# Reordered small loads, value loads, weight halves and last two units, and six added products of ones, in a fused attention and two-MoE kernel

## The chip, the cores and the metric

The kernel runs on one core of one Trainium2 chip. The core has TensorE (PE, with its weight loads shown as a queue of their own, PEld), VectorE (DVE), ScalarE (ACT), GpSimd (POOL) and SyncE (SP), which issues nearly all of the plain DMA transfers here. The metric is device time in microseconds (us), the median over several executions.

## The reference

Three stages follow each other. All data is float32.

- Attention: q, k, v are [4 batches, 8 heads, 576 positions, 64]. Two attentions are added: one over positions averaged in groups of four (144 by 144, repeated to 576), and a local one in which a position sees those less than 4 away.
- First MoE (soft): with x = [2304, 512], `logits = x @ phi` (32 slots, 8 experts of 4 slots). A softmax over the 2304 rows mixes tokens into slots, each expert applies `relu(s @ w1[e]) @ w2[e]` (512 to 1024 to 512), and a softmax over slots mixes the results back.
- Second MoE (top 2 of 8): `x @ w_gate + log1p(exp(x @ w_noise)) * noise`, the best two experts of each token, a softmax over the two, and `out[token] += weight * (relu(x @ w1[e]) @ w2[e])`.

Each MoE has weights of 8 experts, two matrices of 2 MB per expert: 32 MB for each MoE.

## The kernel before, in words

**Attention by units.** A unit is one batch and two heads: 16 units, numbered 0 to 15. A software pipeline runs over p = -1 to 14. In step p the names of the list `SEQ` are called in order, each for the unit p minus its offset, so a unit's work is spread over several steps. What matters here: `ld` (line 187) loads k and q of unit p+2, four transfers of 144 KB; `A0`, `A1` (231) transpose k and q of unit p+1 on PE; `S` (284) makes the local scores of unit p, `SD` (298) the coarse ones; `M EL EX SU P0 P1` and `MD DX RD DM` are the two softmaxes; `VD` (267) averages the values of unit p-1; `CP`, `CD` transpose the probabilities; `DP` (408) and `DD` (420) multiply with the values; `XA`, `EP`, `LG`, `LA` add, transpose and make the router logits of unit p-2. `lV` (203) loads the values of unit p+1, mostly four transfers of 80 KB, into one of three buffers in turn. Every instruction order is written out by hand (`manual_schedule`): an engine runs its own instructions in the order in which the program calls them.

**The tail.** Units 13 to 15 are finished by the list `TSEQ`, with unit numbers written out (`DD:13`), which ends in the softmax over slots (`SE SK MT M4 SS ST MB QW QS UA DN UB SI`) and a few products of ones (`H2`, `H1`). `cp` (223) moves results from PSUM to SBUF, on DVE where the name is listed in `ON_V` (in the tail `ON_V_END`), else on ACT.

**Weights of the first MoE.** They are fetched during attention and after it. The 16 matrices go in the order `ORDW`. The first eight are loaded in steps 1 to 14: each matrix is four transfers of 512 KB, queued in a list, and at each name `W` (two per step) `NW[p]` of them are issued: 1 in steps 1 to 12, 2 in steps 13 and 14. The name `R2` in the tail (630) opens the second ring: three more matrices into space that the attention's own tiles leave, w8 and w10 (second matrices of an expert, in quarters: 8 transfers of 256 KB each) and w9 (a first matrix, 4 of 512 KB). A tile of the ring can be loaded when the attention tiles that lay there have been read for the last time. The last five matrices go into buffers of the first matrices once PE has used them (726 to 728). Then SP goes on to the second MoE's weights and to clearing the output (`clear`, 113).

SP issues all this from one queue, in program order. Ahead of the names of steps 13 and 14 stand four `small` loads each (596): the gate weights (`wgn`) and the noise (`nz`), in rows of 32 bytes.

**First MoE** (lines 794 to 857): `hidden`, `hidden_t`, `second` for eight experts on PE, accumulating in `yacc`.

**Second MoE.** After the router, DVE ranks the tokens and makes one-hot tiles `oh` (921). `dispatch` (934) multiplies them with the stacked token data `stk` into `xs0` and `xs1`. For expert 0 the first `NOH` = 10 dispatches run ahead of the expert's matmuls (1228), then `spin` (1089, products of ones that nothing reads), then `gathered` copies `xs0`, then first layer (1042) and `tile2` (1062), 24 matmuls of 512 columns for each 128 tokens. The weights of the second matrix are split in two parts, `whi` (ACT) and `wlo` (DVE), and so is the hidden layer, `hh` and `hl`.

Of the kernel before, what the change touches and what calls it, by code (L numbers as in the profile page):

```python
# [15 lines left out]

CAP = 640

SEQ = """ld DM S DD A0 M a00 a01 A1 W a110 XA a100 SD EL a101 ST a111 SK CP SS EX W VD EP01 MD V0 EP00 EP10 SU_ LG CD
EP11 EP V1 LA ED0 DX SU KD ED1 DP lV x1 x0 DQ1 X0 SE DQ0 RD P0 X1 P1""".split()  # L20
TSEQ = """S:15 DD:13 XA:13 DM:14 CP:14 W EP01:14 EP00:14 SD:15 M:15 EL:15 EP10:14 EX:15 EP11:14 CD:14 ED0:14 MD:15 SU:15 VD:14 DP:14 V0:14 V1:14 EP:13
ED1:14 P0:15 P1:15 DD:14 DX:15 LG:13 X0:13 RD:15 x0:14 DM:15 x1:14 CP:15 LA:13 EP00:15 X1:13 EP01:15 EP11:15
CD:15 EP10:15 XA:14 ED0:15 VD:15 DP:15 V0:15 V1:15 ED1:15 DD:15 EP:14 x0:15 x1:15 LG:14 X0:14 XA:15 LG:15 EP:15 X0:15 LA:14
LA:15 SE:3 X1:14 SK:2 H2 MT M4 X1:15 SS:3 H2 ST:3 MB R2 QW QS UA DN UB H1 SI H2 SK:3""".split()

ON_V = ['k1', 'd1', 'a101', 'a111', 'v0']
ON_V_END = ['P0', 'k1', 'v0', 'v1']

NW = [0] + [1] * 12 + [2] * 2

# [1 line left out]
NPRE = 8  # L32
NHOT = [4, 8]
N2 = 3
# [4 lines left out]
def attn_moe_moe_kernel(ctx: ExitStack, tc: tile.TileContext, q, k, v, moe_phi, moe_w1, moe_w2,  # L39
                        w_gate, w_noise, noise, w1, w2, out, dbg=None):  # L40
    nc = tc.nc
    B, H, S, D = q.shape
    NT = B * S
    DM = H * D
# [11 lines left out]
    NU = len(units)  # L56
# [13 lines left out]
    onesb = const.tile([128, 128], BF, name="onesb")  # L70
# [48 lines left out]
    with ExitStack() as tctx:  # L119
# [62 lines left out]
        def tp():  # L182
            return ps.tile([128, 512], F32, name="t", bufs=4)

        LD, KD, DQ, SD, SS, SB, PD, PL, XL, XT, XK = ({} for _ in range(11))
# [32 lines left out]
                    if j1 < 5:  # L218
                        nc.sync.dma_start(out=V[64:121, 4, h], in_=hv[h, S - 57:S])

        TAIL = []

        def cp(name, dst, src, alt=False):
            if name not in (ON_V_END if TAIL else ON_V) and not alt:
                nc.scalar.activation(dst, src, AF.Copy)  # L225
            else:
                nc.vector.tensor_copy(dst, src)
# [70 lines left out]
        def b_d(u):  # L298
            kd = KD.pop(u)
            sd = ps.tile([128, 512], F32, name="Sd")  # L300
            if u == 1:
                hot(NHOT[1], sd)
            for qb in range(3):
                nc.tensor.matmul(sd[0:96, qb * 144:qb * 144 + 144], Dq[:, qb].rearrange("p h i -> p (h i)"), kd,  # L304
                                 start=True, stop=True, skip_group_check=True)
            SD[u] = sd

        def soft_m(u):
            m = wka.tile([128, NG], F32, name="m")
# [128 lines left out]
        ET_ = {}  # L438
# [22 lines left out]

        def logit_pe(u):
            xT, kk = XT[u], u % 4
            L = SB[u + 2][:, 0:192] if not TAIL else ET_[u][1][:, 128:320] if u in ET_ else tp()[:, 0:192]
            for t in range(4):
                nc.tensor.matmul(L[32 * t:32 * t + 32, 0:128], phi[:, kk], xT[:, 128 * t:128 * t + 128],
                                 start=True, stop=True, skip_group_check=True)
            for t in range(4):
                nc.tensor.matmul(L[32 * t:32 * t + 32, 128:192], phi[:, kk], xT[:, 512:576], start=True, stop=True,
                                 skip_group_check=True)  # L470
            LL[u] = L

# [100 lines left out]
        MW, todo = {}, []  # L573

        def mload(i, pool, names=("wr", "wr")):
            MW[i], go = wload((moe_w1, moe_w2)[i % 2][i // 2], (4, 8)[i % 2], pool, names)
            if i == 2 * E - 1:
                go = [lambda f=f, c=c: f(ks=(c, c + 2)) for c in range(2) for f in go]
            todo.extend([lambda f=f, c=c: f(whole=c) for f in go for c in (1, 2)] if len(MW) <= NPRE else go)

        def flush(n=99):
            for _ in range(min(n, len(todo))):
# [2 lines left out]
        for i in range(NPRE):  # L585
            mload(ORDW[i], ringa if i < 3 else ringb)
        small = [(wgn[:, :, E * i:E * i + E], w.rearrange("(k p) e -> p k e", p=128))
                 for i, w in enumerate((w_gate, w_noise))]
# [4 lines left out]
        for p in range(-1, NU - 1):  # L593
            if p == 0:
                nc.sync.dma_start(out=phi, in_=moe_phi.rearrange("(k p) s -> p k s", p=128))
            for _ in range(4 if p >= NU - 3 else 0):
                o, i = small.pop(0)
                nc.sync.dma_start(out=o, in_=i)
            if p == 1:
                nc.gpsimd.memset(zero, 0.0)  # L600
            b4, r4 = divmod(p - 5, 4)
            for nm in SEQ:
                f, off, a = BL.get(nm, (None, 99, ()))
                if off is None:
                    if 0 <= b4 < B and r4 == a:
                        f(b4)
                elif ok(p - off):
                    f(p - off, *a)
                if nm == "W" and p >= 0:
                    flush(NW[p])  # L610
                if p == -1 and nm == "lV":
                    nc.gpsimd.memset(PT, 0.0)
                    nc.gpsimd.memset(Vd[:, 1], 0.0)
                    nc.gpsimd.memset(PdT[:, 1], 0.0)
                if p == -1 and nm == "DQ1":
                    nc.vector.memset(P, 0.0)
            if p == 0:
                hot(NHOT[0])
                nc.vector.tensor_scalar(trib, jp, 0.0, None, op0=ALU.is_gt)
                consts()  # L620
# [58 lines left out]
        for nm in TSEQ:  # L679
            if nm in TB:  # L680
                TB[nm]()
            elif nm[0] == "H":
                hot(int(nm[1:]))
            else:
                n, u = nm.split(":")
                f, off, a = BL[n]
                f(int(u), *(a if off is not None else ()))


# [244 lines left out]
    def dispatch(e, n):  # L934
        i = ORD[n]
        lo, hi = WIN[i]
        if n == 0:
            XP[e] = [ps.tile([128, n], F32, name=f"xs{c}", bufs=1) for c, (_, n) in enumerate(CH)]
        oh = OH.pop((e, n))
        c1 = CH[1][0]  # L940
        if lo < c1:
            nc.tensor.matmul(XP[e][0][:, lo:min(hi, c1)], stk[:, i], oh[:, 0:min(hi, c1) - lo], start=(n == 0),  # L942
                             stop=True, skip_group_check=True)
        if hi > c1:
            nc.tensor.matmul(XP[e][1][:, max(lo, c1) - c1:hi - c1], stk[:, i], oh[:, max(lo, c1) - lo:hi - lo],  # L945
                             start=(i == FIRST1), stop=True, skip_group_check=True)
# [139 lines left out]
        if (e, ti) in DRAINS:  # L1086
            nc.gpsimd.drain()  # L1087

    def spin(n):

        t = ps.tile([128, DM], F32, name="y") if n else None
        for _ in range(n):
            nc.tensor.matmul(t, onesb, onesb[:, None].to_broadcast([128, 4, 128]), start=True, stop=True)


    ELSE = {}
# [12 lines left out]
    with ExitStack() as gctx:  # L1109
# [13 lines left out]
        t = ps.tile([128, 2 * E], F32, name="h")  # L1123
# [9 lines left out]
        for q_ in range(5):  # L1133
            n = min(4, NTILE - 4 * q_)
# [69 lines left out]
        for i in range(NTILE - 1):  # L1204
            n = NTILE - 1 - i
# [21 lines left out]
            wsplit(0, kk, "v", (1,))  # L1227
        for n in range(NOH):
            dispatch(0, n)
        spin(SPIN[5])  # L1230
        gathered(0, (0,))
        if PLP is None:
# [178 lines left out]
```

## Time and profile before

| | us |
|---|---|
| three runs, median (lowest to highest) | 491.67 (491.55 to 493.74) |
| the profiled execution | 490.25 |
| span of its trace | 488.5 |
| PE busy, share of the span | 462.5, 95% |
| DVE, ACT, POOL busy | 275.3, 270.5, 220.1 |

Attention runs to about 158 us, the first MoE to about 193, the router to 204, and the rest is the second MoE. In tables by stage, the columns are the stretch, its length, busy us and instruction counts of PE, PEld, DVE, ACT and POOL, then the granted TensorE clock as a share of 2.4 GHz, the mean busy share of the 16 DMA engines (it can pass 1.00), and GB/s. In a timeline a row is the start, us, engine, line, operation, destination and source, the count, and in brackets the idle time before it with what ended it. SPq is SP's queue; its rows show when a transfer is issued, not when it lands.

### The profile page before, as it was taken

The numbers are of one execution on the slowest core, as the hardware profiler recorded it, in microseconds if no ns is written. First come the engines' busy times: TensorE is split into PE (matmuls) and PEld (weight loads), VectorE is DVE, ScalarE is ACT, GpSimd is POOL, SyncE is SP. The second block draws the span as 40 slices with busy tenths as digits, with TensorE's granted clock in tenths as the row PEclk, the third lists the DMA queues.
The fourth block names the chain that finished last, engine by engine and source line by source line (L and its number), as shares of the span: only waits on it lengthen the run. The fifth ranks groups of instructions, "written<-read, shape, count | busy, mean of one in ns | idle before, by whom it ended". The sixth has DMA issues, their size and how long they took to land.

```text
span 488.5 us, 12466 instructions
## 1 busy us (share of the span) xinstructions
PE 462.5 (95%) x4765; PEld 358.7 (73%) x4765; DVE 275.3 (56%) x703; ACT 270.5 (55%) x699; POOL 220.1 (45%) x321
## 2 busy tenths in 40 slices
PE   6999999899789999999999999999999999999992
PEld 5798788788575443577777887887887877878882
DVE  6888878878575321876578464383552634615300
ACT  2688877778483112665384464682755646727410
POOL 7898777678331001084556577322222222212232
PEclk9999999999799999979999999999999999999998
DMA  8999999999989999999977843799867855333333
GB/s 163 213 208 257 213 245 216 205 264 186 251 250 333 397 389 395 375 345 335 377 186 203 230 68 67 190 363 280 273 88 214 214 127 144 45 43 45 44 44 46
DMA packets 108233, 104.19 MB, mean 213 GB/s; under 512 B 67978, under 2 KB 77898, under 8 KB 108170
## 3 DMA queue, kind: packets, MB, share of 16 engines
q1 hardware_dynamic: 101258, 90.50, 62.5%
q0 software_dynamic: 6912, 12.85, 17.5%
q8 instruction: 40, 0.66, 0.6%
q14 instruction: 23, 0.19, 0.1%
HBM read 83.60 MB, written 19.73 MB: 212 GB/s over the span
## 4 chain that ended last, share of the span: by engine, by line
PE 58%; DMA 16%; issue 12%; SPq 3%; DVE 3%; ACT 3%; POOL 2%; POOLq 2%; ACTq 0%; DVEq 0%
PE y L1062 35%; DMA wr<-in_moe_w_dram 7%; DMA ld<-in_q_dram 5%; SPq L192 3%; PE t L237 3%; PE gx L879 2%; PE S L293 2%; PE h L1042 2%; PE Sd L304 2%; POOL out_dram L1081 2%; DMA V<-in_v_dram 2%; DMA w10b<-in_moe_w_dram 1%; POOLq L1087 1%; PE gx L1042 1%; PE xs L942 1%
## 5 line engine op out<-in xcount | busy, mean ns | idle before, releaser
L1062 PE MATMUL y<-whi,hh 128*128 128x512 f32 x320 | 127.6, 399 | 0.3 <-ACT hh L1043 0.3
L1062 PE MATMUL y<-whi,hl 128*128 128x512 f32 x320 | 127.7, 399 | 0.0
L1062 PE MATMUL y<-wlo,hh 128*128 128x512 f32 x320 | 127.3, 398 | 0.0
L1081 POOL DMA_INDIRECT out_dram<-ys,idx x40 | 63.9, 1597 | 110.3 <-ACT ys L1073 61.2
L1073 ACT ACTIVATE ys<-y,gt 128x512 f32<-128x512 f32 x40 | 27.4, 685 | 82.4 <-issue 47.1
L1062 PEld LDWEIGHTS y<-wlo,hh 128*128 128x128 f32 x320 | 60.5, 189 | 13.0 <-issue 0.8
L1034 DVE TENSOR_TENSOR wlo<-wr,whi 128x512 fp32r<-128x512 f32 x64 | 42.0, 692 | 49.5 <-ACT whi L1031 38.0
L1062 PEld LDWEIGHTS y<-whi,hh 128*128 128x128 f32 x320 | 60.7, 190 | 12.0 <-ACT hh L1043 0.6
L1062 PEld LDWEIGHTS y<-whi,hl 128*128 128x128 f32 x320 | 60.6, 189 | 11.5 <-issue 2.1
L1008 POOL DMA_INDIRECT tab<-stk,pos x36 | 35.8, 994 | 11.5 <-issue 10.4
L1044 DVE SCALAR_TENSOR_TENSOR hl<-h,hh 128x256 fp32r<-128x256 f32 (+1 forms) x64 | 31.3, 490 | 16.5 <-ACT hh L1043 14.3
L1044 DVE SCALAR_TENSOR_TENSOR hl<-gx,hh 128x256 fp32r<-128x256 f32 (+1 forms) x64 | 31.3, 488 | 11.1 <-ACT hh L1043 8.5
L1031 ACT ACTIVATE whi<-wr 128x512 fp32r<-128x512 f32 x64 | 36.9, 625 | 0.2
L1043 ACT ACTIVATE hh<-gx 128x256 fp32r<-128x256 f32 (+1 forms) x64 | 28.1, 439 | 16.0 <-PE gx L1042 13.2
L1043 ACT ACTIVATE hh<-h 128x256 fp32r<-128x256 f32 (+1 forms) x64 | 27.9, 436 | 13.5 <-PE h L1042 10.7
L237 PE MATMUL t<-idf,ld 96*128 96x96 f32 x192 | 23.5, 271 | 10.8 <-DMA ld<-in_k_dram 7.3
L1080 POOL MEMSET spacer<- 1x1 f32 x40 | 13.6, 339 | 42.4 <-issue 42.4
L255 POOL TENSOR_TENSOR s<-Q 64x288 f32<-64x288 f32 x31 | 29.3, 944 | 2.4
L237 PEld LDWEIGHTS t<-idf,ld 96*128 96x128 f32 x192 | 18.8, 154 | 15.0 <-issue 6.2
L337 POOL TENSOR_TENSOR P<-El,su 64x350 f32<-64x350 f32 x31 | 24.4, 786 | 11.3 <-DVE su L330 5.4
L225 ACT ACTIVATE PT<-t 64x384 f32<-64x384 f32 (+1 forms) x64 | 25.9, 428 | 3.1 <-PE t L379 1.9
L927 DVE TENSOR_TENSOR oh<-iot,R 128x256 fp32r<-128x256 f32 (+2 forms) x50 | 20.7, 447 | 11.5 <-PE xs L945 7.8
(312 smaller groups left out, 882.3 us busy)
## 6 DMA issues: line engine op xcount, KB each, us to landing
wr<-in_moe_w_dram SPq DMA_DIRECT2D x72, 512.0 KB
wr<-in_moe_w_dram SPq DMA_DIRECT2D x88, 256.0 KB
out_dram<-zero SPq DMA_DIRECT2D x20, 256.0 KB
V<-in_v_dram SPq DMA_DIRECT2D x62, 80.0 KB
ld<-in_k_dram SPq DMA_DIRECT2D x32, 144.0 KB
ld<-in_q_dram SPq DMA_DIRECT2D x32, 144.0 KB
XT<-tab SPq DMA_DIRECT2D x5, 320.0 KB
tab<-zero SPq DMA_DIRECT2D x6, 256.0 KB
```

Source lines behind the costliest of these rows:

```text
L225: nc.scalar.activation(dst, src, AF.Copy)
L237: nc.tensor.transpose(t[:, 96 * c:96 * c + 96], ld[:, i, 3 * j + c].rearrange("p h d -> p (h d)"), idf[0:96, 0:96])
L255: nc.gpsimd.tensor_tensor(q2, q4[:, :, 0:2], q4[:, :, 2:4], op=ALU.add)
L337: eng.tensor_tensor(P[as_, :, HQ * a:HQ * a + KW], El[as_], su[as_, :, None].to_broadcast([64, NG, KW]), op=ALU.mult)
L1008: st = nc.gpsimd.indirect_dma_start(out=tab, out_offset=bass.IndirectOffsetOnAxis(ap=pos[:, c, i:i + 1], axis=0), in_=stk[:, i].bitcast(F3 ...
L1031: nc.scalar.activation(whi[:, kk], wb(kk), AF.Copy)
L1034: eng.tensor_tensor(wlo[:, kk], wb(kk), whi[:, kk].bitcast(F32), op=ALU.subtract)
L1043: nc.scalar.activation(hh[:, f], h, AF.Relu)
L1044: nc.vector.scalar_tensor_tensor(hl[:, f], h, 0.0, hh[:, f].bitcast(F32), op0=ALU.max, op1=ALU.subtract)
L1062: nc.tensor.matmul(y, l[:, kk, ts_], r_[:, kk], start=(m == 0), stop=(m == 23))
L1073: nc.scalar.activation(ys, YS.pop((e, ti)), AF.Copy, scale=gt[:, ti:ti + 1])
L1081: st = nc.gpsimd.indirect_dma_start(out=out, out_offset=bass.IndirectOffsetOnAxis(ap=idx[:, ti:ti + 1], axis=0), in_=ys, in_offset=None, c ...
```

## The change

- In each step `lV` moves from behind `DP` to behind `A1`; the first `W` moves from behind `A1` to behind `CD`. SP's order in a step was k and q, weights, weights, values; it becomes k and q, values, weights, weights.
- The `small` loads of steps 13 and 14 move from ahead of the step's names to behind them.
- w8 and w10 are loaded in halves of a tile (512 KB) where they were loaded in quarters (256 KB): 12 transfers for the second ring where there were 20.
- `TSEQ` has another order. The logits of units 13 to 15 are put into the score banks `S` and `Sd` instead of the `t` buffers. The evacuations on DVE in the tail are listed by name and unit: `v1` (units 14, 15) goes to ACT; `p10`, `d1` and `x0` of unit 15 go to DVE.
- `spin` takes a width; behind each of the dispatches 4 to 9 of expert 0 stands one product of ones of 128 columns.

```diff
-SEQ = """ld DM S DD A0 M a00 a01 A1 W a110 XA a100 SD EL a101 ST a111 SK CP SS EX W VD EP01 MD V0 EP00 EP10 SU_ LG CD
-EP11 EP V1 LA ED0 DX SU KD ED1 DP lV x1 x0 DQ1 X0 SE DQ0 RD P0 X1 P1""".split()
-TSEQ = """S:15 DD:13 XA:13 DM:14 CP:14 W EP01:14 EP00:14 SD:15 M:15 EL:15 EP10:14 EX:15 EP11:14 CD:14 ED0:14 MD:15 SU:15 VD:14 DP:14 V0:14 V1:14 EP:13
-ED1:14 P0:15 P1:15 DD:14 DX:15 LG:13 X0:13 RD:15 x0:14 DM:15 x1:14 CP:15 LA:13 EP00:15 X1:13 EP01:15 EP11:15
-CD:15 EP10:15 XA:14 ED0:15 VD:15 DP:15 V0:15 V1:15 ED1:15 DD:15 EP:14 x0:15 x1:15 LG:14 X0:14 XA:15 LG:15 EP:15 X0:15 LA:14
-LA:15 SE:3 X1:14 SK:2 H2 MT M4 X1:15 SS:3 H2 ST:3 MB R2 QW QS UA DN UB H1 SI H2 SK:3""".split()
+SEQ = """ld DM S DD A0 M a00 a01 A1 lV a110 XA a100 SD EL a101 ST a111 SK CP SS EX W VD EP01 MD V0 EP00 EP10 SU_ LG CD W
+EP11 EP V1 LA ED0 DX SU KD ED1 DP x1 x0 DQ1 X0 SE DQ0 RD P0 X1 P1""".split()
+TSEQ = """DD:13 W S:15 CP:14 SD:15 EP01:14 XA:13 EP11:14 VD:14 M:15 EP00:14 EL:15 EX:15 EP10:14 MD:15 V0:14 V1:14 DM:14 CD:14
+SU:15 EP:13 DP:14 P0:15 ED0:14 ED1:14 X1:13 DX:15 P1:15 RD:15 DD:14 x0:14 CP:15 x1:14 LG:13 DM:15 X0:13 XA:14 EP11:15
+EP01:15 EP10:15 EP00:15 VD:15 CD:15 V0:15 V1:15 DP:15 ED1:15 ED0:15 LA:13 DD:15 x1:15 LG:14 EP:14 x0:15 XA:15 LG:15
+LA:14 X0:14 LA:15 SE:3 EP:15 X1:14 X1:15 X0:15 SK:2 H2 MT M4 SS:3 H2 ST:3 MB R2 QW QS UA DN UB H1 SI H2 SK:3""".split()
...
-ON_V_END = ['P0', 'k1', 'v0', 'v1']
+ON_V_END = ['P0', 'k1:13', 'v0:14', 'p10:15', 'd1:15', 'v0:15', 'x0:15', 'k1:14', 'k1:15']
...
-            SD[u] = sd
+            SD[u] = SB["d"] = sd
...
-            L = SB[u + 2][:, 0:192] if not TAIL else ET_[u][1][:, 128:320] if u in ET_ else tp()[:, 0:192]
+            L = (SB[min(u + 2, NU - 1)] if u < NU - 1 else SB["d"])[:, 0:192]
...
-            todo.extend([lambda f=f, c=c: f(whole=c) for f in go for c in (1, 2)] if len(MW) <= NPRE else go)
+            todo.extend([lambda f=f, c=c: f(whole=c) for f in go for c in (1, 2)] if len(MW) <= NPRE + N2 else go)
...
-            for _ in range(4 if p >= NU - 3 else 0):
-                o, i = small.pop(0)
-                nc.sync.dma_start(out=o, in_=i)
...
+            for _ in range(4 if p >= NU - 3 else 0):
+                o, i = small.pop(0)
+                nc.sync.dma_start(out=o, in_=i)
             if p == 0:
                 hot(NHOT[0])
...
-    def spin(n):
+    def spin(n, w=4):
...
-            nc.tensor.matmul(t, onesb, onesb[:, None].to_broadcast([128, 4, 128]), start=True, stop=True)
+            nc.tensor.matmul(t[:, 0:128 * w], onesb, onesb[:, None].to_broadcast([128, w, 128]), start=True, stop=True)
...
             dispatch(0, n)
+            spin(int(n > 3), 1)
         spin(SPIN[5])
```

## Rows read from the trace of the kernel before

**Rows 1.** Busy time, clock, DMA share and GB/s by stage, late attention and first MoE.
```profile
100.00:120.00 20.00, 19.10 (x377) 17.05 (x378) 16.23 (x43) 16.14 (x51) 15.16 (x24) 1.00 1.10 241
120.00:124.00 4.00, 3.22 (x96) 2.68 (x93) 3.83 (x12) 3.51 (x16) 3.46 (x5) 1.00 0.51 81
124.00:132.00 8.00, 5.95 (x45) 5.26 (x49) 3.60 (x8) 3.62 (x10) 2.63 (x5) 0.60 1.08 316
...
134.00:138.00 4.00, 4.00 (x114) 3.44 (x106) 3.71 (x10) 2.69 (x10) 1.67 (x3) 1.00 0.51 146
...
144.00:150.00 6.00, 3.72 (x80) 2.75 (x78) 1.39 (x5) 3.14 (x9) 0.90 (x2) 1.00 0.69 218
...
156.00:168.00 12.00, 12.00 (x212) 6.56 (x213) 4.70 (x17) 1.55 (x4) 2.66 (x23) 1.00 1.03 399
...
186.00:192.00 6.00, 6.00 (x29) 1.52 (x28) 0.19 (x1) 0.00 (x0) 1.95 (x3) 1.00 1.05 396
```

**Rows 2.** Timeline of the last expert's `yacc` and the first `hidden`, on PE.
```profile
158.22 2.15 PE L801 MATMUL hp<-wr,sinT 128*32 128x256 f32 x36
...
186.61 6.14 PE L825 MATMUL yacc<-wr,hz 128*32 128x512 f32 x21
```

**Rows 3.** Who waited for whom on PEld, over the whole span.
```profile
PEld yacc L825 <- DMA wr<-in_moe_w_dram: 5.3, 8, 1.2
```

**Rows 4.** Timeline of SP's queue, steps 13 and 14 and the second ring.
```profile
117.56 0.60 SPq L598 DMA_DIRECT2D wgn<-in_moe_w_gate_dram  x1
...
118.76 1.20 SPq L598 DMA_DIRECT2D nz<-in_moe_noise_dram  x2
120.06 2.52 SPq L192 DMA_DIRECT2D ld<-in_k_dram  x2
...
123.73 2.03 SPq L103 DMA_DIRECT2D wr<-in_moe_w_dram  x4
126.17 3.25 SPq L213 DMA_DIRECT2D V<-in_v_dram  x4
129.47 5.22 SPq L598 DMA_DIRECT2D nz<-in_moe_noise_dram  x4
134.73 2.16 SPq L103 DMA_DIRECT2D wr<-in_moe_w_dram  x4
136.99 2.65 SPq L213 DMA_DIRECT2D V<-in_v_dram  x4
...
140.26 6.96 SPq L105 DMA_DIRECT2D w8a<-in_moe_w_dram  x4
```

**Rows 5.** Who waited for whom on SP's queue, 118 to 162 us.
```profile
SPq L105 <- DMA wr<-in_moe_w_dram: 4.0, 2, 2.1
```

**Rows 6.** Timeline of PE where it waits for k, q and values.
```profile
125.27 0.86 PE L237 MATMUL t<-idf,ld 96*128 96x96 f32 x6 [2.06 <-DMA ld<-in_k_dram]
126.91 1.19 PE L237 MATMUL t<-idf,ld 96*128 96x96 f32 x6 [0.78 <-DMA ld<-in_q_dram]
...
146.63 0.65 PE L274 MATMUL xa<-V,four 128*32 128x128 f32 x16 [1.21 <-DMA V<-in_v_dram]
```

**Rows 7.** The same columns by stage: step 12, step 14, the tail.
```profile
106.00:113.30 7.30, 7.30 (x160) 6.58 (x159) 6.24 (x16) 6.06 (x20) 5.71 (x10) 1.00 1.11 245
...
121.20:136.06 14.86, 12.03 (x184) 9.55 (x176) 8.74 (x24) 8.04 (x29) 5.16 (x9) 0.77 0.84 208
136.06:158.20 22.14, 19.51 (x329) 14.02 (x322) 13.63 (x45) 12.12 (x39) 6.31 (x26) 1.00 0.92 311
```

**Rows 8.** The same columns for the expert 0 dispatch and first tile.
```profile
207.57:214.22 6.65, 6.34 (x18) 4.88 (x19) 5.63 (x11) 3.89 (x10) 6.09 (x8) 0.50 1.02 343
```

**Rows 9.** Busy time of DVE alone, from the last one-hot to the last `hl`.
```profile
207.28:217.04 9.76, 8.46 (x18) 0.65 1.03 345
```

**Rows 10.** Timelines of PE and DVE at the dispatch: products of ones, one-hots.
```profile
198.57 3.19 PE L1093 MATMUL y<-onesb 128*128 128x512 bf16 x14
...
203.72 3.64 DVE L927 TENSOR_TENSOR oh<-iot,R 128x128 fp32r<-128x128 f32 x10
...
204.44 1.98 PE L942 MATMUL xs<-oh,stk 128*128 128x128 f32 x6 [0.17 <-POOL stk L1222]
```

More of the change, by code (lines that the diff above doesn't have):

```diff
@@ L219, in load_v @@
                         nc.sync.dma_start(out=V[64:121, 4, h], in_=hv[h, S - 57:S])
-        TAIL = []
+        TAIL, TU = [], [0]
         def cp(name, dst, src, alt=False):
-            if name not in (ON_V_END if TAIL else ON_V) and not alt:
+            if (f"{name}:{TU[0]}" not in ON_V_END if TAIL else name not in ON_V) and not alt:
                 nc.scalar.activation(dst, src, AF.Copy)
@@ L686, in attn_moe_moe_kernel @@
                 f, off, a = BL[n]
+                TU[0] = int(u)
                 f(int(u), *(a if off is not None else ()))
```

## The prediction

> **What bounds the kernel now.** I first read the table by stage, to see which engine or queue each stretch is full of. Through step 13 the DMA engines are full: share 1.10 at 241 GB/s from 100 to 120 us. Then come three holes, 120 to 124 (0.51), 134 to 138 (0.51) and 144 to 150 (0.69), and from 156 us the share is 1.03 to 1.05 at 396 to 399 GB/s until the first MoE is over [rows 1]. Next I read who ends the first MoE. PE starts it at 158.22, and its last stretch of `yacc`, 6.14 us from 186.61, is stretched by weights that come late: PE's weight loads waited 5.3 us for them, eight times [rows 2, 3]. From 158.22 to 186.61 PE worked 28.4 us almost without a wait; the end at 186.61 + 6.14 = 192.7 is the DMA stream's, not PE's. What shortens that stream shortens the kernel, since the router and the second MoE follow in a chain.
>
> Third comes SP's queue, to see why the stream has holes [rows 4]. From 117.56 to 119.96 SP issues four small loads, only then the last k and q (120.06); from 129.47 four more small loads hold it for 5.22 us; the values of unit 15 go out at 136.99, behind four 512 KB weights issued at 134.73; the four quarters of w8a take 6.96 us to issue, with two waits of about 2 us each for earlier weights to land [rows 5]. SP thus waits on landings, and a queue filled with small transfers has few bytes under way. Last, PE: it waits 2.06 and 0.78 us for the last k and q and 1.21 us for the values of unit 15 [rows 6]. Behind the first of these waits the clock is at 0.60 on average over 124 to 132 us, that is mostly at 1.2 of 2.4 GHz [rows 1], and step 14 takes 14.86 us where step 12 took 7.30 [rows 7].
>
> **The change, part by part.**
>
> *Small loads behind the steps.* In step 13, 120.06 - 117.56 = 2.5 us of SP's time come out ahead of the last k and q [rows 4]; all else ahead of these is the same, as they are first in the step in either order. They then land some 2.5 us sooner, against a wait of 2.06 + 0.78 = 2.8 us [rows 6]. The small loads still have to be issued, now behind four weights of 512 KB, 2.1 MB, or 2.1 / 0.396 = 5.3 us of stream that covers them [rows 1].
>
> *Values ahead of weights.* Unit 15's values now go out ahead of the weights of step 14, so the wait of 1.21 us [rows 6] should go. A value load must wait for its buffer, last read three units earlier. For the earlier steps I count nothing: the stream is full there and carries the same bytes. If SP did stand at such a wait in each step, the stream would lose that time; this is a rival below.
>
> *Halves for the second ring.* 20 transfers become 12, all of 512 KB. Their price on the stream I take as nothing by size: at 186 to 192 us, in pieces of 256 KB, it runs at 396 GB/s, at 156 to 168, with 512 KB among them, at 399 [rows 1]. What they buy is bytes under way while SP waits on landings [rows 5]: this is the hole at 144 to 150. [...]
>
> *The sum of the stream.* The holes hold 4.0 x 0.49 + 4.0 x 0.49 + 6.0 x 0.31 = 5.8 us of DMA time [rows 1]. In the new order I still see one thin place, in step 14: four small loads and five of values stand between two groups of 2.1 MB, and SP must wait for the first group to land. I leave 1.0 us there, about half of one hole of 2.0 us. So 5.8 - 1.0 = 4.8 us are gained; from below the bound is nothing (all holes come back elsewhere), from above 5.8.
>
> *The tail.* Its new order matters only if it becomes the bound. The step of 14.86 us can come down by at most 14.86 - 7.30 = 7.6 us, and the tail of 22.14 by the 1.21 us wait [rows 6, 7]. PE could start the first MoE at about 150. With the stream's end at 192.7 - 4.8 = 187.9, PE must start by 187.9 - 28.4 = 159.5, later than today; so the tail has room for many more microseconds. A tighter limit is the first reuse of a weight buffer: matrix 12 is loaded where matrix 1 was, so PE's first `hidden`, 2 us, must be done before the stream runs dry. The stream would reach it about 5 us earlier than now; a start by 155 or so keeps this free. Moved evacuations (three to DVE, two to ACT, each below 0.5 us) and logits in other PSUM banks lie inside the same room; I count nothing, and at most 1.2 us either way, the size of the one wait there is.
>
> *Products of ones.* One product of 512 columns takes 3.19 / 14 = 0.228 us at the full clock [rows 10], so 128 columns take a quarter, 0.057, and six take 0.34; at half the clock 0.68. They stand between dispatches that come at the pace of DVE's one-hots, 3.64 / 10 = 0.36 us each, while six dispatches start within 1.98 us, 0.33 each [rows 10]: some of it falls into gaps. I take 0.2 us, between 0 and 0.7. Against that, the clock falls right at the end of these dispatches: it is 0.50 from 207.57 to 214.22 [rows 8]. If it stayed at 1.00, half of 6.34 busy us would go on PE, 3.2 us, but DVE makes `wlo` and `hl` for the same matmuls and is busy 8.46 of 9.76 us there [rows 9]. It can be shortened by its idle 9.76 - 8.46 = 1.3 us and no more. So the gain lies between 0 and 1.3; I take 1.3, since before the fall the only thin stretch is the dispatch itself, and it is the later part that is filled.
>
> The sum is 4.8 + 1.3 - 0.2 = 5.9 us. The profiled execution took 490.25 (span 488.5), so the changed kernel would take 484.35 as that execution; the median of the runs lies 491.67 - 490.25 = 1.4 above, so 485.8.
>
> **The rivals.**
>
> *Stream gained, clock not held.* The products thicken the dispatch by a third at most, and the clock falls all the same: 485.8 + 1.3 = 487.1. For it speaks that PE waits for ACT right behind the dispatches too, which nothing fills. [...]
>
> *The holes move.* In the new order SP waits elsewhere, for example at w9 and w10, whose space unit 15 must leave: if that is as late as now (unit 15's last value products are at about 148 to 149 us), the stream goes dry there once the 4 MB of w8 and w9 are through. Of 4.8 us some 1 to 2 remain, and the ones add their 0.2: 490 to 491. Against it speaks that unit 15's k and q come sooner.
>
> *Values hold up SP in every step.* This is the case on the slower side. If the value load finds its buffer still in use, the weights and the next k and q wait behind it on SP. The steps from 50 to 120 us run with the DMA engines full, so each microsecond that SP stands idle long enough to drain them is lost. Over some 8 such steps, 0.7 us per step would eat the gain of 5.9, and from 1.1 us per step on the kernel is slower by more than 0.5%: at 1.1, 485.8 + 8.8 = 494.6. Against it: the buffer is free from the end of the step before, and before the change these loads go out without a long wait.
>
> **How the numbers follow.** Stream and clock 0.40 (485.8); stream without clock 0.33 (487.1); holes move 0.14 (490.5); values hold up SP, or the tail turns out as the bound, 0.09 (494.6); more than the sum, with the thin place gone and a shorter tail, 0.04 (about 483). This kernel's runs differ by up to 0.4%, so 0.5%, 2.5 us, is about what can be told from no change. Faster by that (below 489.2): 0.40 + 0.33 + 0.04 = 0.77 less 0.02 for a holes case in between, 0.75; within it 0.16; slower 0.09. The range leaves out the slower case and the far end of the gain: from 5.8 + 1.3 + 1.2 = 8.3 us of gain, 483.4, rounded out to 482.5, to no change, 491.5. The likeliest case alone spans 484 to 487.5.
>
> **What would show it.** Right: SP's row of the last k and q starts near 117.5; step 14 is near 8 us; no wait of PE for values; no stretch of 4 us between 120 and 156 with a DMA share under 0.8; `yacc` ends near 188; clock 1.00 from 207 on, moved by 5 us. Wrong: a share under 0.9 before 118 us (SP held up); holes at w9 or w10; an earlier `hidden` with `yacc` still ending at 192; the clock falling behind the dispatches as before.

## The result and the profile after

The changed kernel takes 493.52 us (median of 20, 488.87 to 495.99), the kernel before 489.38 (20 runs, 485.1 to 493.74). The ratio is 1.0071, interval 1.0046 to 1.0095: slower by 0.7%, where 485.8 us was predicted. The two profiled executions happen to be alike, 490.35 after and 490.25 before; so the profile shows where time moved, and medians say how much it is worth. The profiled execution of the changed kernel is 3.2 us below its median, one of the fastest of its 20.

The stages of the changed kernel, in the columns of [rows 1]:

```profile
100.00:120.00 20.00, 20.00 (x447) 17.48 (x443) 17.24 (x47) 16.16 (x53) 15.51 (x24) 1.00 0.89 205
120.00:124.00 4.00, 4.00 (x65) 3.62 (x62) 3.86 (x9) 3.19 (x8) 3.16 (x5) 1.00 0.96 295
124.00:132.00 8.00, 7.41 (x150) 6.38 (x148) 7.27 (x19) 6.97 (x26) 6.06 (x10) 1.00 1.03 236
...
134.00:138.00 4.00, 2.27 (x57) 1.76 (x57) 3.65 (x10) 2.67 (x10) 2.39 (x3) 1.00 0.70 147
138.00:144.00 6.00, 6.00 (x130) 5.16 (x127) 3.62 (x11) 4.01 (x15) 1.07 (x2) 1.00 0.74 224
144.00:150.00 6.00, 5.59 (x126) 4.13 (x124) 3.73 (x9) 3.70 (x10) 1.16 (x2) 1.00 1.02 313
```

Two of the three holes are filled (0.96 for 0.51 at 120, 1.02 for 0.69 at 144), but 138 to 144 us, at 1.11 before, has 0.74, and 100 to 120 us, full before at 1.10 and 241 GB/s, has 0.89 and 205: the sign that the prediction named for its slower rival. SP's queue in the same stretch, to be held against [rows 4]:

```profile
113.03 5.01 SPq L213 DMA_DIRECT2D V<-in_v_dram  x4
118.10 1.88 SPq L103 DMA_DIRECT2D wr<-in_moe_w_dram  x2
120.07 0.93 SPq L192 DMA_DIRECT2D ld<-in_k_dram  x2
121.05 1.06 SPq L192 DMA_DIRECT2D ld<-in_q_dram  x2
122.21 4.90 SPq L213 DMA_DIRECT2D V<-in_v_dram  x4
...
133.72 4.54 SPq L213 DMA_DIRECT2D V<-in_v_dram  x4
```

Four value loads hold SP for about 5 us, where they took 3.25 and 2.65 [rows 4]. So the last k and q go out at 120.07, no sooner than the 120.06 of before, although the small loads no longer stand ahead of them. `yacc` ends at 194.87 (191.56 + 3.31, the last of its rows in PE's timeline) against 192.75 [rows 2], and PE's weight loads there wait 6.8 us for weights, nine times, not 5.3 [rows 3]:

```profile
191.56 3.31 PE L826 MATMUL yacc<-wr,hz 128*32 128x512 f32 x9
```
```profile
PEld yacc L826 <- DMA wr<-in_moe_w_dram: 6.8, 9, 1.2
```

Of these 2.1 us, 1.9 come back at the dispatch. From the first dispatch to the second tile, 11.7 us, the clock stays at full speed; before, it took 13.6 us, and 6.65 us of it had 0.50 [rows 8]. The stage before, then after:

```profile
204.40:218.00 13.60, 13.25 (x48) 10.26 (x49) 12.27 (x27) 10.23 (x25) 8.80 (x14) 0.75 1.04 348
206.60:218.30 11.70, 11.18 (x54) 8.17 (x55) 11.61 (x27) 10.24 (x25) 8.11 (x10) 1.00 0.98 327
```

And there is a loss at the start that the prediction did not have. POOL's fills of zero (`PT`, `Vd`, `PdT`) hang in the code on the name `lV` of step -1, so they moved forward with it. They ran from 7.19 us before and run from 3.88 now, beside DVE's making of `four` and Q, and PE's first scores start at 9.51 us, not 7.59 (timeline of PE):

```profile
9.51 2.35 PE L293 MATMUL S<-K,Q 128*64 128x35 f32 x40 [1.91 <-DVE Q L227]
```

Last, a kind of wait that was small before, 0.5 us in one place of the steps, and now is not. PE stands still in the middle of its products with nothing that releases it ("issue"), and behind the longest such pause the clock falls. First the row of PE's timeline, then the stages around it in the columns of [rows 1]:

```profile
83.27 0.46 PE L417 MATMUL xb<-PT,V 64*64 64x58 f32 x2 [2.02 <-issue]
```
```profile
75.00:81.20 6.20, 6.20 (x123) 5.45 (x119) 5.67 (x13) 4.76 (x16) 3.73 (x6) 1.00 1.17 274
81.20:83.30 2.10, 0.08 (x4) 0.04 (x1) 0.94 (x4) 0.43 (x3) 1.96 (x4) 0.96 0.74 105
83.30:90.00 6.70, 6.70 (x68) 6.15 (x69) 2.29 (x5) 3.02 (x8) 1.22 (x2) 0.50 1.03 254
```

PE is "busy" for all of 83.3 to 90, but with 68 products where the 6.2 us ahead had 123. The clock in these columns is a share of full speed. In the kernel before, products of ones of 512 columns start 215 to 216 ns apart at 1.00 (from 198.57 us), and the closest products of `y`, of 512 columns too, 426 ns apart at 0.50: 2.4 and 1.2 columns per ns, on which the prediction's "1.2 of 2.4 GHz" can stand as an estimate.

### The profile page after: what moved, and what is told of

The parts are those of the page before. It is cut to its first block, busy times and chain, and to the rows that moved or that the text cites. A ratio compares the mean times of both kernels' runs of the same rounds, so it can differ in the third digit from the quotient of the medians.

```text
span 488.6 us, 12455 instructions
## 1 busy us (share of the span) xinstructions
PE 461.2 (94%) x4771; PEld 359.0 (73%) x4771; DVE 277.4 (57%) x704; ACT 269.3 (55%) x698; POOL 221.8 (45%) x321
## 4 chain that ended last, share of the span: by engine, by line
PE 40%; issue 8%; DMA 2%; POOL 2%; POOLq 2%; DVE 1%; ACT 1%; DVEq 0%
PE y L1063 33%; PE gx L880 2%; DMA out_dram<-ys,idx 2%; POOL out_dram L1082 2%; POOLq L1088 1%; PE h L1043 1%; PE gx L1043 1%; PE xs L946 1%; DVE hl L1045 1%; ACT ys L1074 1%; PE xs L1024 0%; PE xs L943 0%; DVE wlo L1035 0%; ACT hh L1044 0%; PE gx L960 0%
## 5 line engine op out<-in xcount | busy, mean ns | idle before, releaser
L337 POOL TENSOR_TENSOR P<-El,su 64x350 f32<-64x350 f32 x31 | 24.2, 781 | 11.3 <-PE t L446 4.8
L928 DVE TENSOR_TENSOR oh<-iot,R 128x256 fp32r<-128x256 f32 (+2 forms) x50 | 20.7, 446 | 11.3 <-PE xs L946 9.5
L293 PE MATMUL S<-K,Q 128*64 128x35 f32 x640 | 23.2, 233 | 3.0 <-DVE Q L227 1.9
```

Of the source, the lines that this page charges most:

```text
L293: nc.tensor.matmul(s[64 * a:64 * a + 64, KW * g:KW * g + KW], Q[:, c0:c0 + 32].rearrange("p i h -> p (i h)"), K[:, c0:c0 + KW], start=Fals ...
L337: eng.tensor_tensor(P[as_, :, HQ * a:HQ * a + KW], El[as_], su[as_, :, None].to_broadcast([64, NG, KW]), op=ALU.mult)
```

## The experiments

Ratios are to the kernel before on the same chip, with the 95% interval. GB/s is that of 38 to 120 us, steps 4 to 12. "Pauses" sums, up to 120 us, the stretches above 0.3 us from the start of one PE instruction to the start of the next, where the next has number 193 + 256 n. All of PE's instructions in the trace count, from 0: products, weight loads and semaphore waits. The time of the instruction itself is in the sum; PE's idle time alone is less, 4.4 us in the changed kernel, 5.5 in e5 and 7.6 in e14. `yacc` is when it ends in the profiled execution.

| kernel | median us | ratio | GB/s | pauses us | `yacc` |
|---|---|---|---|---|---|
| before | 489.38 | 1 | 231 | 1.1 | 192.8 |
| changed | 493.52 | 1.0071 (1.0046, 1.0095) | 219 | 5.1 | 194.9 |
| e1: changed, old SEQ | 486.43 | 0.9932 (0.9909, 0.9956) | 230 | 2.1 | 191.5 |
| e2: changed, fills where they were | 491.83 | 1.0055 (1.0021, 1.0089) | 221 | 5.9 | 192.1 |
| e3: before, new SEQ | 492.66 | 1.0053 (1.0022, 1.0083) | 220 | 7.0 | 194.1 |
| e4: before, ones | 489.35 | 0.9985 (0.9956, 1.0014) | 227 | 3.4 | 195.8 |
| e5: e2, four value buffers | 490.85 | 1.0029 (0.9997, 1.0062) | 217 | 6.7 | 196.8 |
| e6: e1, four value buffers | 486.98 | 0.9951 (0.9919, 0.9984) | 233 | 1.4 | 192.9 |
| e7: e1, values of unit 15 early | 485.31 | 0.9932 (0.9896, 0.9967) | 231 | 1.5 | 191.2 |
| e8: before, small loads, halves, ones | 486.66 | 0.9937 (0.9904, 0.9970) | 228 | 0 | 192.3 |
| e9: e5, weights in pieces | 502.07 | 1.0236 (1.0186, 1.0285) | 203 | 3.6 | 206.4 |
| e10: e5, blocks shifted | 492.21 | 1.0050 (1.0020, 1.0080) | 219 | 3.9 | 194.4 |
| e11: before, small loads | 488.09 | 0.9965 (0.9932, 0.9998) | 230 | 0.7 | 191.8 |
| e12: before, halves | 489.33 | 0.9982 (0.9952, 1.0013) | 229 | 1.1 | 193.9 |
| e13: e5, a weight on each side | 490.07 | 1.0009 (0.9981, 1.0037) | 221 | 1.7 | 192.8 |
| e14: e5, 1 MB transfers | 490.98 | 1.0026 (0.9998, 1.0054) | 218 | 9.3 | 196.0 |
| e15: e7, 1 MB transfers | 485.07 | 0.9897 (0.9861, 0.9934) | 230 | 2.7 | 192.4 |
| e16: e5, no weights in steps | 502.84 (one) | | 135 | 0 | 207.5 |
| e17: e7, four bursts | 485.83 | 0.9946 (0.9908, 0.9984) | 227 | 0 | 188.7 |
| e18: e7, eight bursts | 486.21 | 0.9967 (0.9932, 1.0001) | 233 | 0 | 190.5 |

The last three columns are from one execution each, and those scatter: e4 is the kernel before up to the dispatch, yet its `yacc` ends 3.0 us later. A difference of a few microseconds between two entries of `yacc` shows nothing by itself.

**e1, the changed kernel with the old SEQ.**

```diff
-... A1 lV a110 ... LG CD W / EP11 ... DP x1 ...
+... A1 W a110 ... LG CD / EP11 ... DP lV x1 ...
```


> The changed kernel with only the list SEQ as it was (values behind DP, first W behind A1); small loads behind the steps, halves, the new tail and the products of ones stay. The changed kernel's median lies 4.1 us above the one before. Theory A (the value loads, put ahead of the weights, hold up SP's queue in every step): the loss goes, V groups take 2.7 us of SP again, the DMA share of 38 to 50 us is back at 1.0 and of 100 to 120 us at 1.1, yacc ends 2 us or more before 194.9, and the time is 1.5 to 6 us below the kernel before (its clock term of 1.6 and some of the 4.8 of the stream). Theory B (the loss is in the tail: new order of the last units, small loads and halves): yacc still ends at about 195, and the time stays 2 to 4 us above the kernel before.

486.43 us, V back to 2.65 to 3.63 us per group, 230 GB/s, a share of 1.11 from 100 to 120 us. Theory A holds in its sign and size: in the changed kernel the new SEQ, with the fills that hang on it, costs 1.0071 - 0.9932 = 1.4%, 6.8 us, and the rest of the change gains 0.7% with the old one.

**e2, the fills where they were; e3, SEQ alone in the kernel before.**

```diff
-                if p == -1 and nm == "lV":
+                if p == -1 and nm == "DP":
```


> The changed kernel, with the three fills of zero on POOL (PT, Vd, PdT) hung on DP instead of lV, so that they run where they ran before. Theory C (the loss is at the start: the fills moved forward with lV and run beside the making of the first Q): S of unit 0 starts at 7.6 us where it started at 9.5, everything behind it is 1.9 us sooner, and the time is 1.9 us under the changed kernel. Theory A (SP's queue sets the pace of the steps): S of unit 0 starts at 7.6 too, but by unit 8 or so the steps are as late as in the changed kernel, yacc ends within 0.7 us of 194.9, and the time is that of the changed kernel within 1 us.

The first scores start at 7.68 us. The gain is 0.16% (0.8 us), inside the intervals. `yacc` ends at 192.1, not within 0.7 us of 194.9 as theory A had it, but this execution, 487.13 us, is the fastest of its twelve.

> The kernel before with only the list SEQ of the change (values behind A1, first W behind CD; the fills of zero on POOL go with lV). Theory A: slower by 3 to 6 us (the whole loss of 4.1 and the 1.6 that the products of ones give back), V groups take 3 to 6 us of SP, yacc ends at 195 or later. Theory B: within 2 us of the kernel before (only the start, 1.9 us late). Theory C: slower by 1.9 us, and no more.

Slower by 0.5%, 2.6 us; the new SEQ alone loses, but less than theory A's 3 to 6 us, and `yacc` ends at 194.1, not at 195 or later. Theory C's 1.9 us lies inside the interval too, so this run does not tell the two apart; e2, with 0.8 us, speaks against C. The changed kernel is e3 with the rest of the change, and at 1.0071 against 1.0053 that rest gains nothing, where with the old SEQ it gains 0.7% (e1). So of the 6.8 us some 2.6 are the order's own price, and some 4 are a gain of the other parts that does not come with it.

**e4, the products of ones alone.** The added lines of the diff, in the kernel before.

> The kernel before with only the six products of ones of 128 columns behind the dispatches 4 to 9 of expert 0. Theory D (they hold the clock): the granted clock is 1.00 from 204 to 482 us where it was 0.50 from 207.57 to 214.39, and the time falls by 1.1 to 1.9 us (the 1.9 us that the changed kernel wins between its first dispatch and its first tile of y). Rival: the clock falls all the same, since PE waits for ACT right behind the dispatches, and the time is 0 to 0.7 us longer.

The clock holds, and the dispatch to the second tile takes 11.7 us (before 13.6). At the end 0.15%, 0.7 us, is left, inside the interval. Over all runs, the clock held here in 14 of 16 profiles with these products (it fell in e6 and e9), and fell in each of the four without (before, e3, e11, e12).

**e5, e2 with four value buffers, in the new order; e6, four in the old.**

```diff
-        Vs = [(wk, a1, a2)[i].tile(... for i in range(3)]
+        Vs = [(wk, a1, a2, wk)[i].tile(... for i in range(4)]
-            V = Vs[u % 3]
+            V = Vs[u % 4]
```


> The changed kernel with the fills of zero where they were, and a fourth buffer for the values, so that a value load never waits for PE (its wait for DP three units back is gone); the order on SP's queue stays values ahead of weights. Without the fourth buffer this kernel took 491.83 us, with SEQ as it was 486.43. Theory A1 (it is the wait for the buffer that holds up SP): the rows of V on SP fall to 2.7 us or less, no wait of SP for PE at these loads, the DMA share of 100 to 120 us is back above 1.0, and the time comes down by 4 to 5.4 us, to 486.4 to 488. Theory A2 (it is the order of the transfers itself, small ones behind small ones and the weights late, with or without the wait): 490 to 492.

> The changed kernel with SEQ as it was and four buffers for the values. With three it took 486.43 us and SP's waits for PE at value loads summed to about 11.6 us between 20 and 160 us, 0.4 us each in the mean. Theory A1: these waits cost little where the values go last, since the k and q behind them are two units ahead: within 1 us of 486.43. Rival: every wait of SP costs stream, as in the changed kernel: 1 to 3 us faster than 486.43.

SP's waits for PE at value loads, from 38 to 120 us, sum to 9.7 us before and 26.1 in the changed kernel, and are gone in e5 (one of 2.0 us stands behind 120). But e5 gains 0.26% on e2 (inside the intervals) and moves 217 GB/s. So the buffer, the rival's mechanism, is about a fifth of the 1.2% between e2 and e1, and not told from nothing; the order itself is the rest. In e6 the buffer brings nothing.

Nor do the value loads get shorter, as theory A1 had it: one takes 1.11 us of SP in e5, 1.09 in the changed kernel and 0.63 before (means from 38 to 120 us), while one of k or q takes 0.77, 0.70 and 0.97. What holds SP at the values in e5 is thus not the buffer. A step in SP's timeline, before and in e5:

```profile
70.38 2.65 SPq L213 DMA_DIRECT2D V<-in_v_dram  x4
```
```profile
69.18 4.32 SPq L213 DMA_DIRECT2D V<-in_v_dram  x4
```

**e7, values of unit 15 alone ahead of the weights, else e1; e8, no new tail.** `SEQ15` is the old SEQ with `lV` ahead of the first W; e8 is the kernel before with small loads, halves and ones, by their lines of the diff.

```diff
-            for nm in SEQ:
+            for nm in SEQ if p < NU - 2 else SEQ15:
```

> The changed kernel with SEQ as it was in all steps but the last, in which the values of unit 15 go ahead of the weights. Theory of the prediction for this part (the wait for the values of unit 15, here 2.3 us at the first product of VD in the last step, goes): that wait is gone, the tail is 1 to 2.3 us sooner, and the time lies 0 to 1.5 us under 486.43, as the stream of weights and not PE sets the end of the first MoE. Rival: the weights, 1 MB each step, go out later, and the time is 0.5 to 2 us above 486.43.

> The kernel before with three parts of the change: small loads behind the steps, halves for the second ring, products of ones. SEQ, the order of the last units, the banks of their logits and the list of evacuations are those before. The same kernel with the new order of the last units took 486.43 us, the products alone 489.35, the kernel before 489.24. If the stream sets the end of the first MoE (the prediction's sum) and small loads and halves bring its gain: 486 to 487.5. If the new order of the last units brings it, by letting PE free the first ring's buffers sooner: 488.5 to 490.

PE's wait for these values goes, and `hidden` starts at 153.7 (157.5 in e1), but `yacc` ends at 191.2 (191.5): 0.9932 in both. e8 is within 0.05% of e1, so the new order of the last units, its banks and evacuations are worth nothing that could be told here.

**e11, small loads alone; e12, halves alone**, each by its lines of the diff in the kernel before.

> The kernel before with only the small loads of steps 13 and 14 behind the names of the step. Small loads, halves and products together took 486.66 us where the kernel before took 490.35 on the same chip, the products alone nothing beyond their interval (0.9985). By the prediction k and q of unit 15 land 2.5 us sooner and step 14 is up to 2.8 us shorter, while the stream is as long: S of unit 15 starts at 133.5 (136.2 before), yacc ends 0 to 1.5 us sooner. If the small loads carry the gain: 1.5 to 3 us faster.

> The kernel before with only the second ring's matrices in halves of 512 KB in place of quarters. By the prediction the hole at 144 to 150 us goes (1.9 us of DMA time): yacc ends 1.5 to 2 us sooner, and the time is 1.5 to 2 us below the kernel before. Rival: SP waits for the landings of the weights ahead in either case: within 0.7 us.

In e11 SP reaches the last k 3.2 us sooner than in [rows 4], S of unit 15 starts at 132.8 (136.2 before), and 0.35%, 1.7 us, is gained. SP's timeline in e11:

```profile
116.84 1.76 SPq L192 DMA_DIRECT2D ld<-in_k_dram  x2
118.65 2.42 SPq L192 DMA_DIRECT2D ld<-in_q_dram  x2
```

The halves gain 0.9 us, not told from nothing. The hole at 144 to 150 us goes (share 1.09), but `yacc` ends at 193.9, later than before and not 1.5 to 2 us sooner, so that these halves bring the stream forward is not shown.

**e10, 72 more PE instructions ahead of the steps, else e5.** The products of ones of the first steps get 128 columns, not 512, and are four times as many; `hot` gets a width for that, like `spin`.

```diff
-                hot(NHOT[1], sd)
+                hot(4 * NHOT[1], sd, 1)
-                hot(NHOT[0])
+                hot(4 * NHOT[0], None, 1)
```


> The kernel of four value buffers in the new order, with the twelve products of ones of 512 columns in the first steps made as 48 of 128 columns: 72 more instructions on PE ahead of all others, at about the same PE time. Theory F: PE's pauses end again at instruction numbers of 193 plus a multiple of 256, so at other products than in the kernel of four buffers (its work is 72 further on). Rival (PE waits at these products for something that the profile does not show): the pauses stay at the same products, 72 further on in number. The time is that of the kernel of four buffers within 2 us in either case.

The pauses end again at 193 + 256 n, so at other products. Number 2497 was a product of S in e5 (PE's timeline, first row) and is one of DP in e10 (second):

```profile
73.23 0.48 PE L293 MATMUL S<-K,Q 128*64 128x35 f32 x10 [0.90 <-issue]
```
```profile
73.75 0.33 PE L417 MATMUL xb<-PT,V 64*64 64x58 f32 x4 [1.22 <-issue]
```

This reads as PE having run out of instructions: in the trace a packet of 16 KB on the instruction queue lands 1.3 to 1.8 us ahead of the end of each pause over 1 us.

**e16, no weights in steps 1 to 12, else e5.** The weights are all there, but go out from step 13 on.

```diff
-NW = [0] + [1] * 12 + [2] * 2
+NW = [0] * 13 + [2] * 2
```


> The kernel of four value buffers with no weights in steps 1 to 12; all of them go out from step 13 on, so that the first MoE starts late and the time is 20 to 45 us longer; only the steps are of interest. Theory F: with no weights on the way the packets of PE's instructions land at once, the pauses at the blocks sum to less than 1 us, and S of unit 12 starts at 103 us or sooner (111.8 with four buffers, 104.4 in the order before with four). Rival (the small transfers of values and of k and q delay the packets, or PE waits for something else): 3 us of pauses or more.

No pause, no fall of the clock up to 497 us, S of unit 12 at 101.0 us; the time is 13 us longer than before, not 20 to 45. The instruction packets started 0.7 us in the mean behind the last number 193 + 256 n that PE had begun, at most 1.2 up to step 12 (e5: 2.6 and 5.7). So weights on the way are what makes PE's instructions late here. Late is not always a pause: e8, e17 and e18 have all weights on the way and none.

**e9, weights in pieces of 256 KB between the other loads, else e5.** Each 512 KB transfer becomes two; one goes behind each pair of k loads, of q loads and of value loads (by the same two lines in `load` for unit u - 2 and in `load_v` for unit u - 1). Further down, `go` takes the piece's number.

```diff
+                if 1 <= u - 2 <= 12:
+                    flush(1)
-                    flush(NW[p])
+                    flush(0 if 1 <= p <= 12 else 2 * NW[p])
```


> The kernel of four value buffers in the new order, with the weights of steps 1 to 12 in pieces of 256 KB, one behind each pair of k, q and value loads, where two of 512 KB went out together behind the values. In the profiles so far PE stands still 4, 3, 3 and 4 times for 0.8 to 2 us in the kernels with the values ahead (changed, three fills back, SEQ alone, four buffers), with nothing that releases it, and each of these ends at an instruction whose number is 193 plus a multiple of 256; a packet of 16 KB of PE's own instructions lands 1.3 to 1.8 us ahead of each. These packets came 2.4 to 2.8 us in the mean behind the point at which the block before was begun, against 1.9 to 2.2 in the order before, and the more weights passed in between the later (correlation 0.89). Theory F (PE runs out of instructions, because their load waits for the weights that went out ahead): with no more than 256 KB in one place no packet waits over 3.5 us in steps 1 to 12, PE does not stand still there, S of unit 14 starts at 122 or sooner (128.2 with four buffers), and the time is 486 to 487.5 us. Theory A2 (the order on SP's queue holds back the stream by its landings, whatever PE does): 489.5 to 491.

A miss for both theories: the DMA engines are busier (1.17, 0.93 in e5) and move less (203 GB/s, 217 in e5), and PE waits for instructions and for q (4.8 us from 38 to 120, 0.2 in e5). The stage in e9:

```profile
38.00:120.00 82.00, 72.70 (x1364) 61.55 (x1361) 58.44 (x149) 55.83 (x180) 52.86 (x76) 0.94 1.17 203
```

Pieces of half the size in other places cost 1.0236 - 1.0029 = 2.1%. How much of that is the size and how much the places is not shown.

**e13, one weight on each side of the values, else e5; e14 and e15, the 1 MB of a step in one transfer, on e5 and e7.**

```diff
-... A1 lV a110 ... EX W VD ... CD W
+... A1 W lV a110 ... EX W VD ... CD
```


> The kernel of four value buffers (490.85 us) with one weight of 512 KB ahead of the values and one behind them, where both lay behind. Theory F (PE's instructions wait for weights that lie together): the longest waits of their packets halve to about 3 us, the pauses at the blocks fall from 6.7 us to under 3, and the time comes down by 2 to 4 us. Theory A2 (it counts that a weight stands behind the values): 489.5 to 491.5.

```diff
-            todo.extend([lambda f=f, c=c: f(whole=c) for f in go for c in (1, 2)] ...
+            todo.extend([lambda f=f: f(whole=3) for f in go] if len(MW) <= NPRE else ...
```


> The kernel of four value buffers (490.85 us; values ahead of the weights) with the 1 MB of weights of a step in one transfer in place of two, so that nine transfers make a step and not ten. Theory A2 (SP's limit on transfers under way): more bytes under way, so more MB moved by 120 us than the 25.2 of that kernel, and 487 to 489.5. Theory F: the weights lie together as before, the pauses stay at 5 to 7 us, and the time is within 1.5 us of 490.85.

> The kernel with weights ahead of the values in all steps but the last (485.31 us), with the 1 MB of weights of a step in one transfer. If fewer transfers help the stream where it is not held up: 0.5 to 2 us faster. If the stream is no limit in steps 1 to 12 there: within 0.7 us.

e13 has 1.7 us of pauses and not 6.7, yet gains only 0.2% and moves 221 GB/s; PE waits for q in their place, 5.1 us from 10 to 160. That speaks against the pauses as the cause. e14 is no better than e5 (218 GB/s, 217 in e5), though it has more bytes in each of the transfers that theory A2 counts: in the traces of before and after a transfer of SP waits for the semaphore that it will signal, one of eight in turn, so that no more than eight are under way. e15, on the old order, has the lowest ratio of all, 0.9897, 1.0% below the kernel before; its interval meets that of e7.

**e17 and e18, bursts of PE work in e7.** The edit of e17; in e18 the units are 4 to 10 and 12.

```diff
+            if u in (4, 8, 9, 12):
+                hot(6, sd)
```


> The kernel with weights ahead of the values in all steps but the last (485.31 us, ratio 0.993), with six products of ones of 512 columns (1.4 us of PE by the rows of the first steps) ahead of the coarse scores of units 4, 8, 9 and 12: 5.7 us of PE in steps 4 to 12, about what the pauses take in the kernels with values ahead. If PE's time in the steps carries the loss: 4 to 5.7 us longer, ratio 1.001 to 1.005. If the stream of weights sets the end of the first MoE and PE has room: 0 to 1.5 us longer, ratio 0.993 to 0.996.

> The same with the burst in eight steps (units 4 to 10 and 12): 11.3 us of PE. If PE's time in the steps carries the loss: 9 to 11.3 us longer than 485.31, ratio 1.012 to 1.016. If the stream does and PE has room up to some point: less than twice what four bursts cost above 485.31, or a small cost for four and the rest for eight.

Four bursts stand 0.14% above e7, eight 0.35%; PE's time alone would give 1.2% and 2.3%. Below are a burst in PE's timeline of e18, the stage of steps 4 to 12 in e18, in which PE is never idle, and the same stage in e5:

```profile
41.81 1.46 PE L551 MATMUL Sd<-onesb 128*128 128x512 bf16 x6
```
```profile
38.00:120.00 82.00, 82.00 (x1563) 67.56 (x1562) 64.13 (x163) 61.35 (x201) 57.26 (x84) 1.00 1.10 233
```
```profile
38.00:120.00 82.00, 76.99 (x1469) 66.60 (x1471) 61.53 (x160) 60.15 (x195) 55.53 (x81) 0.94 0.93 217
```

This bounds what the pauses are worth. S of unit 14 starts at 127.2 us in e18 and at 128.2 in e5, nearly as late, but the ratios are 0.9967 and 1.0029, 0.6% apart and clear of their intervals taken together (in the profiled executions `yacc` ends at 190.5 and 196.8). A late PE alone does not cost that; what differs is what the DMA engines have moved by then, 233 against 217 GB/s.

## Why the prediction was wrong

**The step that failed** is "For the earlier steps I count nothing: the stream is full there and carries the same bytes". It carries the same bytes, but later: with the new order the change loses 0.7%, without it (e1) it gains 0.7%. All six kernels with all weights behind the values (changed, e2, e3, e5, e10, e14) move 217 to 221 GB/s from 38 to 120 us, the others with weights ahead in transfers of 512 KB or more 227 to 233. At 231 against 219 that is 12 GB/s over 82 us, 1.0 MB, or 2.5 us at 396 GB/s [rows 1]. The first MoE ends by the stream, as the prediction said, so this should show at `yacc`: 192.0 us in the mean of e1, e6, e7 and e8 (191.2 to 192.9), 194.6 in that of the changed kernel, e2, e5 and e10 (192.1 to 196.8). With a scatter of 3 us between two executions of the same code (before and e4) these 2.6 us agree with the 2.5 and do not prove them. The price of the new SEQ by medians is 1.4% (e1 against the changed kernel), 6.8 us. The profiled executions do not show the rest; those of the changed kernel, e2 and e10 are 2.3 to 4.7 us below their medians, that of e5 is 1.6 above. That it is larger than in the kernel before (2.6 us, e3), because small loads, halves and ones gain nothing with the new order, is in the medians; why is open.

**The rival** "Values hold up SP in every step" had the place and the sign, at 0.09. SP does wait longer at the values, so "the buffer is free from the end of the step before" was wrong, but this mechanism is a small part (e5); its time, 494.6, was near by luck, since the full gain it started from was not there either. I gave it so little because the loads went out "without a long wait" before, which says nothing of the wait in another place of the queue. Why a value load takes SP longer and the DMA engines are less busy with values ahead, once the buffer is free, stays open: neither larger transfers (e14) nor a weight on either side (e13) brought it back.

**The base** of 485.8, "1.4 above" the profiled execution, came from three runs; over 20 runs the kernel before has 489.38, 0.9 below it. The forecast itself is a gain of 5.9 us on the kernel before, where a loss of 4.1 was measured.

**The gain of the stream, 4.8 us**, was right in direction and about twice too large. Small loads and halves gain 1.7 and 0.9 us alone; with the ones they gain 3.1 (e8). The term that was too small is "I leave 1.0 us there": in e1 120 to 124 us still has a share of 0.84 and 138 to 150 us shares of 0.68 and 0.75, 4 x 0.16 + 6 x 0.32 + 6 x 0.25 = 4.1 us. 5.8 - 4.1 = 1.7 is what came, in that one execution.

**Small loads**: right (e11), and lost in the changed kernel, where the values of unit 13 and the weights of their step kept SP until 120.07, ahead of the last k and q.

**The ones**: right in that the clock holds. 1.3 - 0.2 = 1.1 us were forecast; 1.9 came in the trace, 0.7 (not told from nothing) in e4's median. What makes the clock fall is not shown. In the changed kernel it fell to 0.50 behind the pause that ended at 83.27 us; but e3, with 7.0 us of pauses, has 1.00 from 38 to 120 us, and e8, with none, has 0.96. e17 and e18 have no fall up to 477 us, and e7 without bursts has none either.

**Tail and unit 15's values**: "I count nothing" was right (e8), and the wait for these values, 1.21 us before and gone in e7, was worth nothing that could be told; PE waits for weights later anyway (5.0 us at `yacc` in e1).

**Missed**: the fills that hang on the name `lV`, 1.91 us at the start, of which 0.8 (not told from nothing) is left at the end.

## What to carry to other kernels

Where one queue feeds a stream that sets the end, a move of small loads ahead of large ones is a change of every step, also if it is meant for one (here 231 GB/s before and 219 in the changed kernel, from 38 to 120 us); look at GB/s over the steps, not at the waits of the engines, and make the move only where its wait is (e7). Price the pauses of an engine by adding known work to it before they are blamed: here 5.7 and 11.3 us of work on PE (e17, e18) cost 0.14% and 0.35%. Test a part of a change with the other parts in and with them out; here the price of one order was 2.6 us without them and 6.8 with them (e3, e1). And see what else hangs on a name that is moved.

## What was not expected of the hardware

PE's instructions come in packets of 16 KB, which the profile lists among those of the 16 DMA engines: 40 packets and 0.66 MB in the kernel before, 0.6% of the engines' time, one for each 256 of PE's instructions from number 193 on (two in two places). PE can run dry, as I read it: it stood for up to 2.57 us in one place and 7.6 us in all up to 120 us (e14), at numbers 193 + 256 n, and not at all with no weights on the way (e16). There was no such pause in e8, e17 and e18 either, under a full stream (228, 227 and 233 GB/s), but 0.7 to 9.3 us of them in the other kernels with weights on the way.
